# Sparse attention and a hardswish feed-forward block on one core: all engines' operations in another listed order

## The chip, the core and the metric

The kernel runs on one core of a Trainium2 chip. The metric is the time of one execution on the device, in microseconds (us); a lower time is better. The engines are named as the profile names them: PE (TensorE, matmuls), DVE (VectorE), ACT (ScalarE), POOL (GpSimd) and SP (SyncE), the last of which only starts transfers here. PEld is the weight load of PE.

## What is computed

Four batches of eight heads, 768 rows and 64 columns go through an attention over a local window and over one summary per block of 32 keys. Its result is the input of a feed-forward block with 512 inputs, 2048 hidden columns and a hardswish gate. Cut to what matters, the reference is:

```python
# q, k, v: (4, 8, 768, 64); w_in: (512, 2048); w_out: (2048, 512)
k_sum = k.reshape(B, H, 24, 32, D).max(axis=3)
v_sum = v.reshape(B, H, 24, 32, D).mean(axis=3)
scores_l = where(|i - j| < 16, q @ k.T / 8, -1e9)
scores_s = q @ k_sum.T / 8 + log(32)
a = softmax(concat([scores_l, scores_s]))
x = a @ concat([v, v_sum])                    # heads side by side: (3072, 512)
h = x @ w_in
out = (h * clip(h + 3, 0, 6) / 6) @ w_out     # (3072, 512), float32
```

## The kernel before, in words

The rows are worked off in eight tiles of 384 rows, s = 0 to 7: two halves of each batch. Each tile goes through attention (scores, exp, masking, values), is turned into x, and then through sixteen blocks of the first matrix (F) and three blocks of rows of the second (G).

**Nothing is scheduled by loops at run time.** The loops of the program only register operations under short keys such as `F5x2.0`, with the engine, the operation and the operations it depends on. The method `Plan.issue` then walks through the text `ORDER` and emits the operations one after the other. Every engine takes its instructions in that listed order, so `ORDER` alone decides what stands ahead of what in each engine's queue. A suffix `:A` or `:D` chooses ACT or DVE for a copy that either could do. Buffers are given out while the text is read: an operation that needs a new buffer gets the free one that was left longest ago.

```python
for n, token in enumerate(ORDER.split()):
    if token[0] in "~-_=":
        keep(...)                      # matmuls on a constant tile, result unused
        continue
    ...
    b.pool, b.slot = min(((p, s) for p in b.among for s in self.pools[p]), key=lambda x: since[id(x[1])])
    ...
```

The keys that matter below:

- `K0a`, `Q0g`, `V0c`, `Q0wu`: loads of batch 0, issued on POOL: keys (`K02` is twice the size of `K00` and `K01`), the queries of the second half row-wise (`Q00`, `Q01`), values by pair of heads, and the queries of the first half in wide rows. `I..` and `O..` are the two weight matrices, `K1..`, `Q1..`, `V1..` and so on the later batches.
- `c.N`: constants. `c.1` builds the identity matrix on POOL, `c.2` the window on POOL, `c.6` and `c.7` the ones beside the values, `c.8` to `c.11` clear the rows of the values that come from the block before.
- `kP`, `qG`: transposes of keys and queries on PE (lines 391, 420, 441) with their copies on ACT or DVE and the maximum over each block on DVE (line 402).
- `sBPH`: scores and exp (lines 489 and 495 for batch 0, 512 and 520 later) and the masking (lines 497, 521); the second digit is the pair of heads (batch 0) or a group of them, the third the half.
- `uN`: block sums of the values (lines 535 and 553) and their spreading; `hBPX`: copies of values of the block before.
- `v0P`: the values of tile 0 by pair of heads (line 581), scaling (598, 605), transposes (589) and the copy into x. `v4HG` is the second half of batch 0, and `vBHG` batch B: values (623), scaling, and for batch 1 transposes (636). From tile 4 on, x is made in another way: the scaled values are turned in blocks of 32 on DVE (`.3`, line 642, into y), and SP moves them by sixteen transfers (`.4` to `.7` of the group that stands second, line 648) into x. F of a tile waits for all sixteen.
- `FSxN.0` is one block of the first matrix, four matmuls of 384 columns (line 666), `.1` the relu on ACT (line 670), `.2` the gate on DVE (line 671). Three PSUM banks h serve F, so the fourth F waits for the gate of the first. For tile 0 the blocks 0 to 4 are split into four single matmuls.
- `GSTxA.0` to `.3` is one block of rows of the second matrix, four matmuls of 512 columns each (line 683), into one PSUM bank o; `.4` is the copy out and `.5` the store, issued on SP (lines 693, 694). The last block of all is split into halves of columns, and its end is copied half by ACT and half by DVE (lines 699 to 703).
- `~N`, `_N`, `-N`, `=N`: matmuls on the constant tile `idle` (line 782) that fill time on PE: N of 512, 64 or 128 columns, and for `=N` one of N times 64.

Of the kernel before, what the change touches and what calls it, by code (L numbers as in the profile page):

```python
# [37 lines left out]
F0x8.1 F0x8.2 F0x5.1 I0.0 F0x5.2 F0x11.0 F0x1.0 F0x11.1 F0x11.2 F0x1.1 F0x1.2 F0x1.3 F0x1.4 F0x1.5 v410.0 v410.1 F0x7.0 F0x7.1
F0x7.2 v410.2 F0x10.0 F0x10.1 I12.0 F0x13.0 F0x13.1 F0x15.0 F0x15.1 F0x13.2 F0x10.2 v411.3 v411.4:D v410.3 v410.4:A F0x15.2
F0x14.0 F0x14.1 F0x14.2 F0x9.0 F0x9.1 F0x9.2 F0x0.0 F0x0.1 F0x2.0 F0x2.1 K13.0 K10.0 c.12:A F0x0.2 K12.0 K11.0 w10.0 Q1w1.0  # L40
F1x14.0 F1x14.1 F1x14.2 F1x4.0 F1x4.1 F1x4.2 F1x2.0 F1x2.1 F1x2.2 w10.1:D F0x2.2 F0x2.3 F0x2.4 F0x12.0 F0x12.1 F0x12.2 F1x8.0
F1x8.1 F1x8.2 F1x1.0 F1x1.1 F1x1.2 F0x0.3 F0x0.4 F0x0.5 F0x2.5 F1x9.0 F1x9.1 F1x9.2 F1x5.0 F1x5.1 F1x5.2 F1x15.0 F1x15.1 w11.0
w11.2 F1x15.2 w11.3:D Q1w4.0 Q1w2.0 Q1w0.0 w10.2 w10.3:D q6.0 q6.1:A q7.0 q7.1:A F1x7.0 F1x7.1 w11.1:A F1x7.2 F1x12.0 F1x12.1
F1x12.2 O0.0 G02x0.0 Q1w5.0 Q1w3.0 q4.0 q4.1:A q5.0 q5.1:A F1x6.0 F1x6.1 F1x6.2 O1.0 G02x0.1 s100.0 s100.1 s100.3 F1x3.0 w12.0
F1x11.0 F1x11.1 w13.0 w13.2 F1x3.1 F1x11.2 w12.2 w12.1:D O2.0 G02x0.2 s101.0 s101.1 O3.0 F1x10.0 G02x0.3 G02x0.4:A w13.3:D
w13.1:A s101.3 F1x0.0 G00x0.0 G00x0.1 w12.3:D s100.2 s101.2 s100.4 V10.0 h100.0:D F1x10.1 h110.0:A F1x10.2 F1x3.2 s110.0 s110.1
s110.2 s101.4 s110.3 G00x0.2 G00x0.3 G00x0.4:A V12.0 u4.0 h130.0:D h120.0:A F1x0.1 u4.1:D u4.2:A u4.4:D u4.3:D u4.5:D G02x0.5
G01x0.0 G01x0.1 G01x0.2 s110.4 F1x0.2 h111.0:A v100.0 v100.1 v100.2 h121.0:A v101.0 v101.1 v101.2 G01x0.3 G01x0.4:A K20.0 K21.0
K22.0 K30.0 K23.0 w21.0 F1x13.0 F1x13.1 F1x13.2 v100.3 v100.4:A w20.0 w21.3 G12x0.0 w21.2:A v101.3 v101.4:A V22.0 H2.0 h101.0:A
w20.3 G12x0.1 G12x0.2 F2x2.0 F2x2.1 F2x11.0 F2x2.2 F2x11.1 F2x11.2 s111.0 w23.0 s111.3 F2x1.0 F2x1.1 F2x1.2 F2x3.0 F2x3.1 F2x3.2  # L50
F2x15.0 F2x15.1 F2x15.2 Q22.0 w23.3 G12x0.3 s111.1 G12x0.4:A F2x5.0 F2x5.1 h131.0:A F2x5.2 F2x6.0 G10x0.0 s111.2 w22.0 w22.3
s111.4 w23.4:A V20.0 H2.1:A K33.0 F2x13.0 F2x13.1 F2x13.2 G10x0.1 F2x6.1 F2x0.0 F2x0.1 F2x0.2 u5.0 u5.1:A u5.5:A F2x6.2 v110.0
v111.0 v111.1 v111.2 Q30.0 F2x4.0 F2x4.1 F2x4.2 Q21.0 Q23.0 Q20.0 w22.4:A F2x10.0 F2x10.1 F2x10.2 F2x12.0 F2x12.1 w20.1 F2x12.2
w22.2:A v110.1 w21.4:A Q33.0 Q32.0 G10x0.2 G01x0.5 G10x0.3 G10x0.4:A v110.2 F2x8.0 F2x8.1 w21.1 w20.2:A F2x9.0 w20.4:A F2x9.1
F2x9.2 u5.2:D F2x14.0 u5.4:D w23.2:A F2x8.2 v111.3 F2x14.1 v111.4:A G11x0.0 G11x0.1 u5.3:D w22.1 v110.3 v110.4:A F2x7.0 F2x7.1
G11x0.2 F3x14.0 F3x14.1 F2x14.2 F2x7.2 F3x14.2 s200.0 s200.1 w23.1 w21.5:A s200.3 G11x0.3 F3x9.0 F3x9.1 F3x9.2 F3x8.0 F3x8.1
F3x8.2 F3x13.0 Q31.0 K31.0 s200.4 s200.2 G11x0.4:A G11x0.5 G12x0.5 s210.0 s210.3 s210.4 s210.1 s210.2 F3x4.0 F3x12.0 G22x0.0
F3x13.1 F3x13.2 H3.0 v201.0 K32.0 V32.0 w20.5:D F3x4.1 F3x4.2 V30.0 G00x0.5 F3x12.1 v200.0 v200.1 F3x2.0 v201.1 v201.2 v201.3
G22x0.1 F3x0.0 F3x0.1 G22x0.2 G22x0.3 w23.5:A G22x0.4:A F3x12.2 v200.2 v200.3 v201.5 F3x1.0 F3x1.1 F3x1.2 s201.0 w31.0 G20x0.0
v201.4 F3x0.2 F3x2.1 s201.3 F3x2.2 F3x11.0 s201.1 G20x0.1 F3x5.0 F3x11.1 F3x3.0 F3x5.1 F3x11.2 w30.0 F3x5.2 v201.7 F3x15.0  # L60
G20x0.2 F3x15.1 F3x15.2 w30.3 F3x3.1 F3x3.2 w22.5:A w30.4:D s201.4 F3x6.0 F3x6.1 H3.1:A G20x0.3 G20x0.4:A F3x7.0 F3x10.0 G21x0.0
s211.0 F3x7.1 F3x10.1 s201.2 F3x7.2 s211.3 s211.1 F3x10.2 w32.0 F3x6.2 w32.3 s211.4 s211.2 w30.2:A G21x0.1 G21x0.2 G21x0.3
G21x0.4:A u6.0 u6.1:D u6.5:A u6.4:A u6.2:A w31.3 v211.0 v201.6 v210.0 v210.1 v210.2 w31.2:D v211.1 v210.3 v211.2 v211.3 G10x0.5
w31.4:D w33.0 G32x0.0 G32x0.1 G32x0.2 G32x0.3 G32x0.4:A F4x14.0 F4x14.1 F4x14.2 F4x4.0 F4x4.1 w32.2:A F4x4.2 F4x15.0 F4x15.1
F4x15.2 w31.1 G30x0.0 G30x0.1 F4x8.0 F4x8.1 F4x8.2 F4x2.0 F4x2.1 F4x2.2 F4x13.0 G30x0.2 F4x13.1 u6.3:A F4x13.2 w33.3 F4x7.0
F4x7.1 F4x7.2 G21x0.5 G20x0.5 v211.4 F4x6.0 F4x6.1 F4x6.2 v211.7 v211.6 v211.5 w30.1 F4x11.0 F4x11.1 F4x11.2 G30x0.3 G30x0.4:A
G30x0.5 F4x1.0 F4x1.1 w33.2:A F4x1.2 w32.4:D F4x5.0 F4x5.1 F4x5.2 G22x0.5 s300.0 s300.3 s300.1 F4x3.0 F4x12.0 F4x12.1 F4x9.0
F4x3.1 F4x9.1 w31.5:A w33.4:A w33.1 w32.1 F4x9.2 F4x12.2 w32.5:D s300.2 G31x0.0 G31x0.1 G31x0.2 s300.4 F4x3.2 s310.0 s310.3
s310.4 s310.1 s310.2 F4x0.0 F4x0.1 F4x0.2 F4x10.0 G31x0.3 w30.5:A F4x10.1 w33.5:D F4x10.2 v301.0 v301.1 v300.0 v301.2 v300.1
G31x0.4:A G31x0.5 v300.2 v300.3 v301.3 F5x14.0 F5x14.1 v301.5 v301.7 v301.6 v301.4 F5x2.0 G42x0.0 G42x0.1 F5x1.0 F5x1.1 F5x2.1  # L70
G42x0.2 F5x14.2 F5x1.2 F5x2.2 s301.0 s301.3 G42x0.3 G42x0.4:D s301.1 s301.2 F5x6.0 F5x6.1 F5x6.2 F5x4.0 F5x4.1 F5x4.2 F5x3.0
s311.0 s311.3 s311.4 F5x9.0 F5x9.1 F5x9.2 F5x3.1 F5x3.2 s311.1 s311.2 s301.4 G40x0.0 F5x13.0 F5x5.0 F5x5.1 F5x0.0 G40x0.1
F5x13.1 F5x13.2 F5x5.2 F5x0.1 F5x0.2 v310.0 v311.0 F5x10.0 v310.1 v310.2 F5x7.0 F5x7.1 F5x7.2 v311.1 F5x8.0 F5x8.1 F5x8.2
F5x10.1 F5x10.2 G40x0.2 F5x12.0 G40x0.3 G40x0.4:A G42x0.5 F5x15.0 F5x11.0 v310.3 v311.2 v311.3 v311.7 F5x11.1 G32x0.5 G41x0.0
G41x0.1 G41x0.2 F5x11.2 F5x15.1 F5x15.2 F6x14.0 F5x12.1 F5x12.2 F6x14.1 F6x14.2 F6x12.0 F6x12.1 F6x12.2 F6x9.0 F6x9.1 F6x9.2
G41x0.3 G41x0.4:A F6x10.0 F6x10.1 F6x7.0 F6x4.0 F6x4.1 F6x10.2 G52x0.0 F6x4.2 F6x7.1 F6x7.2 F6x8.0 F6x8.1 F6x1.0 F6x8.2 F6x1.1
F6x1.2 F6x0.0 F6x0.1 F6x0.2 G52x0.1 F6x3.0 F6x11.0 F6x11.1 G52x0.2 F6x3.1 F6x3.2 G52x0.3 G52x0.4:D F6x5.0 F6x5.1 F6x11.2 F6x2.0
F6x2.1 F6x5.2 F6x2.2 G51x0.0 F6x13.0 F6x13.1 F6x6.0 F6x15.0 G51x0.1 v311.6 F6x6.1 F6x6.2 F6x15.1 v311.5 v311.4 F7x5.0 F6x15.2
F6x13.2 F7x5.1 F7x5.2 F7x13.0 F7x9.0 F7x13.1 F7x13.2 F7x9.1 F7x9.2 G51x0.2 F7x12.0 F7x12.1 F7x12.2 F7x10.0 F7x10.1 F7x10.2
F7x1.0 G51x0.3 F7x1.1 F7x1.2 G51x0.4:A F7x3.0 G40x0.5 F7x6.0 F7x6.1 F7x6.2 G51x0.5 F7x8.0 F7x8.1 F7x8.2 G62x0.0 F7x4.0 F7x4.1  # L80
F7x4.2 F7x3.1 F7x3.2 F7x2.0 G62x0.1 F7x15.0 F7x2.1 F7x2.2 F7x15.1 F7x15.2 F7x0.0 G62x0.2 F7x0.1 G62x0.3 F7x7.0 F7x7.1 F7x0.2
# [732 lines left out]
```

## Time and profile before

| | before |
|---|---|
| time of three runs, us | 217.43, 216.99, 216.66; median 216.99 |
| span of the profiled execution, first to last instruction, us | 215.4 |
| PE busy, us | 207.6 (96%) |
| DVE busy, us | 162.1 (75%) |
| ACT busy, us | 136.0 (63%) |
| POOL busy, us | 49.7 (23%) |
| PE matmuls, instructions | 2521 recorded |
| mean granted clock of PE | 0.998 of full speed |

The profiled execution has no time of its own beside its span; the median lies 1.6 us above the span. Busy time of PE counts the matmuls on the constant tile too. All times in the views below are counted from the start of the span.

### The profile page before, as it was taken

To read this page: it belongs to the slowest core of one execution; us is meant where nothing else is said; L and a number is where in the kernel's file an instruction comes from. 1 tells how busy PE (TensorE), PEld (TensorE's weight loads), DVE (VectorE), ACT (ScalarE), POOL (GpSimd) and SP (SyncE) were. 2 spreads that over 40 slices of the span, in tenths; PEclk is the share of its full clock that TensorE was granted. 3 is DMA by queue.
4 is the path that set the end of the run, shared out by engine and by line. 5 is a ranking of instruction groups with operands and counts; after the bars stand their busy time and mean duration, and the time that the engine had idled before them with its cause. 6 is when DMAs were issued, how large, how long until landed. Compare 5 with 4: busy or idle time off the path is not lost.

```text
span 215.4 us, 6065 instructions
## 1 busy us (share of the span) xinstructions
PE 207.6 (96%) x2521; PEld 119.9 (56%) x2548; DVE 162.1 (75%) x318; ACT 136.0 (63%) x264; POOL 49.7 (23%) x66
## 2 busy tenths in 40 slices
PE   7999999999999999999999999999999999999993
...
DVE  6889889999899999898899889887865555640021
...
PEclk9999999999999999999999999999999999999999
...
DMA packets 91724, 22.68 MB, mean 105 GB/s; under 512 B 82224, under 2 KB 88752, under 8 KB 91696
## 3 DMA queue, kind: packets, MB, share of 16 engines
...
q1 hardware_dynamic: 29264, 7.80, 15.3%
...
## 4 chain that ended last, share of the span: by engine, by line
PE 82%; SPq 5%; DMA 4%; issue 2%; DVE 2%; POOL 2%; ACT 1%; ACTq 0%; POOLq 0%
PE h L666 36%; PE o L683 29%; PE h L683 5%; SPq L648 4%; DMA first<-in_q_dram 3%; PE S L623 3%; PE S L512 2%; DMA out_dram<-ot 1%; ACT vaug L241 1%; POOL first L305 1%; PE S L636 1%; PE S L666 1%; PE h L581 1%; PE S L489 1%; PE S L553 1%
## 5 line engine op out<-in xcount | busy, mean ns | idle before, releaser
L666 PE MATMUL h<-x,win 128*128 128x384 bf16 x500 | 91.1, 326 | 0.1
L670 ACT ACTIVATE r<-h 128x384 f32<-128x384 f32 x125 | 58.7, 492 | 38.8 <-PE h L666 36.8
L671 DVE SCALAR_TENSOR_TENSOR g<-r,h 128x384 bf16<-128x384 f32 x125 | 65.9, 546 | 22.6 <-ACT r L670 20.0
L683 PE MATMUL o<-wout,g 128*128 128x512 bf16 x309 | 78.0, 379 | 1.9 <-issue 0.8
L666 PEld LDWEIGHTS <-win 128*128 128x128 bf16 x512 | 48.7, 98 | 35.5
L683 PEld LDWEIGHTS <-g 128*128 128x128 bf16 x400 | 38.4, 98 | 37.6 <-issue 0.3
L520 ACT ACTIVATE at<-S 120x768 bf16<-120x768 f32 x24 | 18.6, 810 | 5.5 <-PE S L512 5.4
L241 ACT COPY ot<-o 128x512 f32<-128x512 f32 x17 | 10.0, 587 | 15.4 <-PE o L683 14.2
L521 DVE TENSOR_TENSOR at<-at,mask 96x768 bf16<-96x768 bf16 x24 | 12.6, 549 | 2.0 <-ACT at L520 1.6
L605 DVE TENSOR_TENSOR xn<-S,rc 128x768 bf16<-128x768 f32 x14 | 13.3, 950 | 0.3
L343 POOL DMA_DIRECT2D vaug<-in_v_dram x10 | 11.9, 1194 | 0.4 <-DMA first<-in_k_dram 0.2
L241 DVE COPY ot<-h 128x512 f32<-128x512 f32 x2 | 1.3, 686 | 13.7 <-PE h L683 13.7
L683 PE MATMUL h<-wout,g 128*128 128x256 bf16 (+1 forms) x64 | 11.4, 326 | 0.0
L467 DVE TENSOR_REDUCE red<-kaug 128x24 bf16<-128x768 bf16 x12 | 11.2, 943 | 0.1
L241 ACT COPY vaug<-vaug 32x640 bf16<-32x640 bf16 (+3 forms) x17 | 8.9, 574 | 0.6 <-DMA vaug<-in_v_dram 0.3
L241 ACT COPY vaug<-vs 24x1536 bf16<-24x1536 bf16 x6 | 8.8, 1468 | 0.6 <-DVE vs L241 0.5
L782 PE MATMUL o<-idle 128*128 128x64 bf16 (+2 forms) x70 | 7.5, 287 | 1.1 <-DVE idle L287 1.1
L455 DVE STREAM_TRANSPOSE kaug<-kraw 128x768 bf16<-128x768 bf16 x8 | 8.1, 1025 | 0.3 <-PE S L512 0.3
L623 PEld LDWEIGHTS <-at 120*64 120x64 bf16 x336 | 6.3, 111 | 3.0 <-issue 1.6
...
L642 DVE STREAM_TRANSPOSE y<-xn 128x768 bf16<-128x768 bf16 x8 | 7.6, 965 | 0.2
L512 PEld LDWEIGHTS <-kaug 32*128 32x128 bf16 x576 | 5.3, 92 | 4.4 <-issue 3.6
...
## 6 DMA issues: line engine op xcount, KB each, us to landing
...
vaug<-in_v_dram POOLq DMA_DIRECT2D x6, 384.0 KB, 12.9
...
win<-in_moe_w_in_dram POOLq DMA_DIRECT2D x3, 512.0 KB, 10.0
kraw<-in_k_dram POOLq DMA_DIRECT2D x8, 192.0 KB, 12.4
x<-y SPq DMA_DIRECT2D x64, 24.0 KB, 2.0
first<-in_k_dram POOLq DMA_DIRECT2D x6, 192.0 KB, 12.3
first<-in_q_dram POOLq DMA_DIRECT2D x6, 192.0 KB, 12.3
```

The lines of the kernel that those rows point to most:

```text
L241: {"ACT": nc.scalar.copy, "DVE": nc.vector.tensor_copy, "POOL": nc.gpsimd.tensor_copy}[eng](o, i)
L343: op("POOL", "dma128", lambda: nc.gpsimd.dma_start(out=o[BLK:WIN, a:z, 0:D], in_=rows[:, a:z]), w=[("v", b % 2, c) for c in range(lo, hi)] ...
L467: op("DVE", "max", lambda: nc.vector.tensor_reduce(red.slot[:], w[:, :, BLK:WIN].rearrange("p t (n c) -> p t n c", n=2), axis=AX.X, op=ALU ...
L512: nc.tensor.matmul(X[g // 2].slot[:, g % 2, i * QB:(i + 1) * QB], kaug[2 * u + m][rows, t], qT[rows, 2 * u + m, t * QB:(t + 1) * QB], star ...
L520: op("ACT", "exp", lambda a=a, e=e: nc.scalar.activation(a, X[e].slot[0:KEYS, :, 0:HALF], AF.Exp, scale=scl), r=[X[e]], w=[("at", p, half)])
L521: op("DVE", "masking", lambda m=m: nc.vector.tensor_tensor(m, m, mask[:, low(half):low(half) + HQ].unsqueeze(1).to_broadcast([WIN, 2, HQ, ...
L605: nc.vector.tensor_tensor(o, src[..., 0:D], r.unsqueeze(len(r.shape)).to_broadcast(list(o.shape)), op=ALU.mult)
L623: nc.tensor.matmul(X.slot[64 * c:64 * c + 64, i, m:m + D + 1], a[:, t * QB:(t + 1) * QB], vaug[b % 2][0:KEYS, h, t, 0:D + 1], start=True, ...
L666: nc.tensor.matmul(bank(h)[:, 0:HALF], w_in_sb[:, kt, cols], xt[s].slot[:, kt], start=(kt == 0), stop=(kt == NP - 1))
L670: op("ACT", "relu", lambda: nc.scalar.activation(r.slot[:], bank(h)[:, 0:HALF], AF.Relu, bias=0.5, scale=1.0 / 6.0), r=[h], w=[r])
L671: op("DVE", "gate", lambda: nc.vector.scalar_tensor_tensor(gt[s].slot[:, ft], r.slot[:], 1.0, bank(h)[:, 0:HALF], op0=ALU.min, op1=ALU.mul ...
L683: nc.tensor.matmul(o.slot[:, a:z], gt[s].slot[:, ft, ts * 128:(ts + 1) * 128], w_out_sb[:, ft, a:z], start=(ft == 0), stop=(ft == NFT - 1))
```

## The change

The program's functions are the same. `ORDER` is replaced by another text with the same 960 operations, each once, and 13 filling tokens in both, of other sizes. What differs:

- the loads of batch 0 come in the order K01, Q00, K02, K00, V01, V00, Q0w2, Q0w0, Q0w1, Q01, V02, V03, in place of K00, K01, K02, Q00, Q01, V00 to V03, Q0w0 to Q0w2; the identity is built after the window and not before it;
- all constants, copies and steps of tile 0 are interleaved in another way; every F of tile 0 now stands behind all of x of that tile;
- the two value steps of batch 0's second half, `v411.0` and `v410.0`, stand next to each other on PE; before, four F stood between them;
- fewer matmuls on the constant tile: 9 of 512 columns in place of 19, 13 of 128 in place of 15, and 40 of 64 in both;
- 53 copies, spreads and clears change sides between ACT and DVE;
- the sequence of F and G in all tiles, and where the stores and the moves of x stand on SP, are different.

The text has one line more, so that line numbers of the changed kernel are one higher. The diff, cut to the places named here and in the prediction:

```diff
-c.0 K00.0 c.7 c.17 c.6 c.8:A K01.0 c.10:D c.5 c.1 _40 -15 k0.0 k0.2:A c.18 ~1 =2 k1.0 K02.0 ~12 =3 k2.0 k3.0 c.15:D c.2 c.3
-s000.0 k0.3:A c.13:D c.4 c.11:A k1.1 Q00.0 q0.0 k1.4 k0.1 c.20 k1.2:A Q01.0 ~2 =5 q1.0 k0.4 k1.3:D c.9:A c.14:A c.19 k2.3:A
...
-s021.1 s011.1 s021.2 v03.4 v03.5:D s011.2 v02.5:A s031.0 s031.1 s001.0 s031.2 I2.0 F0x3.0 F0x3.1 F0x3.2 F0x3.3 F0x3.4 F0x3.5
-I4.0 F0x6.0 F0x6.1 F0x6.2 F0x4.0 F0x4.1 F0x4.2 F0x4.3 v411.0 v411.1 F0x5.0 F0x4.4 F0x4.5 v411.2 s001.1 I8.0 u0.2:A s001.2 F0x8.0
...
+c.0 c.18 K01.0 Q00.0 K02.0 c.2 c.4 c.1 _40 -13 k1.0 k1.2:A c.3 K00.0 c.6 V01.0 ~1 =6 q0.0 c.19 c.10:A c.11:A k1.3:A c.20 q0.2:A
+k1.1 c.17 q0.1:D V00.0 ~5 =4 k2.0 k3.0 s010.0 k2.2:A c.9:A k2.1 k1.4 c.5 k0.0 s010.1 k0.1 k0.4 s010.2 k3.2:A k2.3:A k0.3:A
+k0.2:D c.16 c.8:D s030.0 k3.1 Q0w2.0 Q0w0.0 Q0w1.0 ~1 =5 s000.0 Q01.0 V02.0 V03.0 I4.0 I8.0 I12.0 k3.3:A h000.0:D =7 s000.1
+u0.0 u0.3:A h010.0:D u0.1:A u0.4:D s000.2 ~1 =7 q3.0 v01.0 k2.4 v01.1 q3.1:D q2.0 I2.0 s021.0 k3.4 v01.2 q2.1:D v01.3 q1.0
+q1.2:D v00.0 v00.1 v01.4 s030.1 h001.0:A s021.1 h011.0:A s020.0 q1.1:D v00.2 s020.1 s030.2 s020.2 v01.5:D v00.3 I0.0 Q1w4.0
+K11.0 K10.0 Q1w2.0 Q1w5.0 h020.0:D c.7 u1.0 u1.1:A u1.3:A v00.4 v02.0 v02.1 s001.0 s031.0 h021.0:A h030.0:D s031.1 u1.4:D v03.0
+v03.1 v02.2 v02.3 u0.2:D v02.4 s011.0 v03.2 v03.3 s001.1 v02.5:A v00.5:D v03.4 v03.5:D ~1 =4 F0x7.0 F0x6.0 F0x5.0 u1.2:D s021.2
+s011.1 h031.0:A s031.2 s001.2 K12.0 K13.0 Q1w3.0 F0x7.1 s011.2 F0x6.1 F0x7.2 F0x6.2 F0x5.1 v411.0 v410.0 v411.1 F0x5.2 v411.2
...
+G31x0.4:A s310.3 s310.4 s310.2 F4x7.0 F4x15.0 G42x0.0 F4x7.1 F4x8.1 v211.4 v300.0 v301.0 F4x7.2 F4x8.2 v301.1 F4x15.1 G42x0.1
+F4x14.0 F5x0.0 F5x0.1 w30.5:A v300.1 v301.2 F4x14.1 w33.5:A v300.2 w31.5:A F4x15.2 F5x0.2 F4x14.2 v300.3 G42x0.2 F5x2.0 F5x14.0
+F5x2.1 s311.0 s311.1 F5x14.1 F5x9.0 G32x0.5 G20x0.5 F5x2.2 v301.3 F5x14.2 F5x9.1 F5x9.2 G42x0.3 F5x15.0 G42x0.4:A F5x11.0
+F5x8.0 G30x0.5 F5x15.1 G40x0.0 F5x11.1 s311.3 s301.0 F5x8.1 F5x15.2 F5x8.2 F5x4.0 s301.3 F5x4.1 F5x4.2 G40x0.1 F5x11.2 s301.1
+s311.2 G40x0.2 v301.7 v301.4 G31x0.5 F5x13.0 G40x0.3 F5x13.1 s301.4 s311.4 s301.2 F5x12.0 F5x12.1 v311.0 F5x13.2 G40x0.4:A
+G42x0.5 v311.1 v311.2 v310.0 F5x5.0 F5x5.1 F5x5.2 F5x12.2 F5x3.0 F5x3.1 F5x3.2 G41x0.0 F5x1.0 F5x6.0 F5x6.1 F5x6.2 F5x1.1
+F5x1.2 v310.1 v311.3 G41x0.1 v301.6 v301.5 F6x12.0 F6x6.0 F6x12.1 F6x6.1 F6x6.2 F6x12.2 v310.2 v310.3 G41x0.2 G41x0.3 G41x0.4:A
...
```

More of the change, by code (lines that the diff above doesn't have):

```diff
@@ L38 @@
[L38 to L81, printed above, removed]
@@ new lines @@
+v03.1 v02.2 v02.3 u0.2:D v02.4 s011.0 v03.2 v03.3 s001.1 v02.5:A v00.5:D v03.4 v03.5:D ~1 =4 F0x7.0 F0x6.0 u1.2:D s021.2 F0x5.0
+s011.1 h031.0:A s031.2 s001.2 K12.0 K13.0 Q1w3.0 F0x7.1 s011.2 F0x6.1 F0x7.2 F0x6.2 F0x5.1 v411.0 v410.0 v411.1 F0x5.2 v411.2
+F0x11.0 Q1w0.0 F0x11.1 F0x11.2 F0x9.0 F0x9.1 F0x9.2 F0x8.0 v410.1 v411.3 F0x15.0 F0x13.0 v411.4:A F0x2.0 F0x2.1 F0x2.2 v410.2
+v410.3 F0x2.3 F0x15.1 Q1w1.0 F0x15.2 F0x13.1 F0x8.1 F0x13.2 F0x8.2 F0x14.0 F0x3.0 F0x3.1 F0x2.4 F0x2.5 F0x14.1 F0x14.2 F0x3.2
@@ new lines @@
+F0x10.0 F0x1.0 v410.4:A F0x3.3 F0x10.1 F0x3.4 F0x1.1 F1x11.0 c.14:A F0x4.0 F0x4.1 O0.0 F0x4.2 F0x1.2 F1x11.1 F0x3.5 F0x10.2
+F1x11.2 F0x1.3 F0x4.3 F0x4.4 F1x13.0 F0x4.5 F1x13.1 F1x13.2 F1x3.0 F1x14.0 O1.0 F0x1.4 F0x1.5 F1x3.1 F1x14.1 F1x14.2 F1x3.2
+F0x0.0 F1x9.0 F0x0.1 F1x9.1 F0x0.2 F0x0.3 O2.0 O3.0 F1x1.0 F1x9.2 F0x0.4 F1x1.1 F0x0.5 F1x1.2 F1x10.0 F0x12.0 F0x12.1 F1x10.1
+q6.0 q7.0 w11.0 F0x12.2 w10.0 F1x10.2 V12.0 F1x7.0 F1x8.0 G02x0.0 F1x5.0 q6.1:A F1x7.1 F1x8.1 F1x8.2 c.15:A w11.1:A F1x0.0
```

44 lines of the change are left out of this document (36 added, 8 removed).

## The prediction

> **What bounds the kernel now.** I read the page first: busy times, the slices, the granted clock.
>
> ```profile
> span 215.4 us, 6065 instructions
> PE 207.6 (96%) x2521; PEld 119.9 (56%) x2548; DVE 162.1 (75%) x318; ACT 136.0 (63%) x264; POOL 49.7 (23%) x66
> PE   7999999999999999999999999999999999999993
> DVE  6889889999899999898899889887865555640021
> PEclk9999999999999999999999999999999999999999
> ```
>
> PE is full in all slices but the first and the last, at full clock; DVE is nearly full for the first 28 slices (150 us). So I asked when PE gets to its main work and whether it waits afterwards: the timeline of PE around the first F, and what PE waited for from 24.3 us to the end; the last two rows, from the chain of waits, give the step from one matmul to the next in a full stream.
>
> ```profile
> 1.13 3.92 PE L782 MATMUL o<-idle 128*128 128x64 bf16 x55 [1.13 <-DVE idle L287]
> 21.32 0.26 PE L581 MATMUL h<-vaug,at 96*64 96x65 bf16 x5 [0.31 <-issue]
> 24.39 2.12 PE L666 MATMUL h<-x,win 128*128 128x384 bf16 x12
> 26.45 0.47 PE L623 MATMUL S<-vaug,at 120*64 120x65 bf16 x18
> PE o L683 <- issue: 0.8, 5, 0.2
> PE S L623 <- issue: 0.3, 1, 0.3
> 119.78 1.73 PE o L683 x8
> 121.51 1.95 PE h L666 x12
> ```
>
> The first F starts at 24.39. After it PE never waits for another engine or a transfer: only 1.1 us of "issue" are left. One F (four matmuls of 1.95/12 = 0.1625) takes 0.65, one part of G (four of 1.73/8 = 0.216) 0.86. I compared the two listed orders at that point: ahead of the first F stand the same operations of PE (all key and query transposes of batch 0, its eight scores, two sums, all four values of tile 0), and behind it the same 282, without filling in either. The result is therefore the shift of the first F, plus new waits behind it, minus switches saved. Before has nearly nothing to lose there, so a gain must come from the start, and each clash the new order has is a loss.
>
> **The start.** Each transfer's issue (timeline of POOL, or the chain of waits) and its time to landing:
>
> ```profile
> 1.36 1.42 POOL L305 DMA_DIRECT2D first<-in_k_dram  x2 [0.84 <-POOLq L798]
> first<-in_k_dram POOLq DMA_DIRECT2D x1, 192.0 KB, 3.4
> 3.32 0.73 POOL L305 DMA_DIRECT2D first<-in_k_dram  x1
> first<-in_k_dram POOLq DMA_DIRECT2D x1, 384.0 KB, 5.4
> 4.76 1.34 POOL L312 DMA_DIRECT2D first<-in_q_dram  x2
> first<-in_q_dram POOLq DMA_DIRECT2D x1, 192.0 KB, 5.7
> 5.43 7.02 DMA first<-in_q_dram
> 8.90 1.03 POOL L343 DMA_DIRECT2D vaug<-in_v_dram  x1
> vaug<-in_v_dram POOLq DMA_DIRECT2D x1, 192.0 KB, 8.3
> 12.73 0.88 POOL L325 DMA_DIRECT2D qwide<-in_q_dram  x1 [0.58 <-DMA first<-in_q_dram]
> qwide<-in_q_dram POOLq DMA_DIRECT2D x1, 128.0 KB, 7.0
> ```
>
> Landings of before (issue plus time to landing) are K00 4.8, K02 8.7, Q00 10.5, Q01 12.4, V03 17.2, last of Q0w 19.7: one stream, so its steps can be put in another order. Between K00 and K02 lie K01 and K02, three shares of 192 KB in 3.9: K01 1.3, K02 2.6. Q00 costs 1.7 to 1.8, Q01 2.0, a V 1.2, all of Q0w 2.5. In the new order: K01 4.8, Q00 6.5, K02 9.2, K00 10.4, V01 11.6, V00 12.8, Q0w 15.3, Q01 17.3, V02 18.5, V03 19.7. The last values come 2.5 us later, the wide queries 4.4 us earlier.
>
> From there I walked the new order forward by hand, with these durations beside the matmul rows (the groups of instructions; the copies have PE to ACT or DVE handoffs of some 0.05):
>
> ```profile
> L402 DVE TENSOR_REDUCE red<-h 128x24 bf16<-128x768 bf16 x3 | 2.8, 949 | 0.4 <-PE h L391 0.4
> L495 ACT ACTIVATE at<-S 120x768 bf16<-120x768 f32 x8 | 6.3, 810 | 1.2 <-PE S L489 1.1
> L282 DVE MEMSET vaug<- 32x768 f32 x3 | 2.1, 698 | 0.4 <-issue 0.2
> L241 ACT COPY vaug<-vaug 32x640 bf16<-32x640 bf16 x6 | 4.3, 717 | 0.0
> L605 DVE TENSOR_TENSOR xn<-h,rc 128x384 bf16<-128x384 f32 x4 | 2.1, 555 | 0.1
> 17.67 0.85 PE L535 MATMUL o<-vaug,ind 96*32 96x128 bf16 x24
> ```
>
> Keys 2 and 3 are transposed from 9.3 to 10.2. DVE then has their and key 0's maxima, the block indicators, a copy of key 0 and the clear `c.8` (0.95+0.95+0.7 and 1.6 of copies), to 14.1, and `u0` needs that clear: 14.2 to 15.0 on PE. Q3, the values of pair 1, Q2, a score, then Q1 (landing 17.3) to 18.0, the values of pair 0 to 18.6, three scores to 19.75. V03 has landed at 19.7: `u1` to 20.6. Behind it stand five short steps and two scores, to 22.1; the values of pair 3 to 22.7; ACT comes to the last exps and copies (eight of 0.7 to 0.8 since 15.6) at 24.0, DVE scales (0.56) to 23.5; the last transpose ends at 23.85 and its copy at 24.2. The first F would start at 24.3. One "issue" gap like the 0.31 at 21.32 fits into such a stretch, so I take 24.6: **+0.2**. Its bounds are 23.7 (V03 at 19.7 plus 4.0 of steps that can't overlap) and 25.8 (each of some twenty handoffs 0.06 slower than taken).
>
> **Switches.** Twelve matmuls of F from 24.39 at 0.1625 each end at 26.34, and the values start at 26.45: 0.11 for going to the other layout, the same for going back. `v411` and `v410` side by side save one pair: **−0.2**.
>
> **The moves of x.** Here the new order is tight. These rows are of tile 6: value steps, turns on DVE, sixteen moves on SP, first F; then three gates in a row, a store between moves, and the moves' landing.
>
> ```profile
> 136.24 0.95 PE L623 MATMUL S<-vaug,at 120*64 120x65 bf16 x48
> 139.52 1.84 DVE L642 STREAM_TRANSPOSE y<-xn 128x768 bf16<-128x768 bf16 x2
> 141.42 11.13 SPq L648 DMA_DIRECT2D x<-y  x16
> 159.19 2.11 PE L666 MATMUL h<-x,win 128*128 128x384 bf16 x12
> 157.34 1.48 DVE L671 SCALAR_TENSOR_TENSOR g<-r,h 128x384 bf16<-128x384 f32 x3
> 160.54 0.61 SPq L694 DMA_DIRECT2D out_dram<-ot  x1
> L648 SPq DMA_DIRECT2D x<-y x16: 591/618/1194, 141.4 to 151.9; - x16
> DMA to landing us min/median/max: 2.0/2.0/3.2
> ```
>
> Before: values end at 137.19, y is ready at 141.4, the last move starts at 151.9 and lands at 153.9, F starts 5.3 later. After: between the values of tile 6 and its first F stand 15 F, 9 parts of G and the same rest, in place of 16 and 11; at 0.65 and 0.86 that is 22.0 − 2.4 = 19.6 us until PE is there. DVE has four gates (two more if `F4x7` and `F4x8` are late) among the scalings and turns: 4.2 + 4×0.465 = 6.1, or 7.0. SP has two stores (`G31`, `G42`) between the moves: 10.5 + 1.2, and 2.0 to land. Sum 19.8 to 20.7, against 19.6: F waits 0.2 to 1.1, I take **+0.5**. The bounds are 0 (SP's moves at 0.66 as in other tiles and handoffs hidden) and 1.6 (a store's bytes ahead of a move, 3.2 in place of 2.0). By the same count tile 5 has 1 to 2 us to spare, tiles 4 and 7 two. [...]
>
> **Elsewhere.** I counted the DVE work listed ahead of each thing that PE needs from the first F on against PE's own work ahead of it: DVE never falls behind in either order, so single clashes remain. At `v100`, 5.0 us of PE work stand behind `u4`, and 4.2 us of DVE work plus handoffs. I take **+0.2** for all of these, from 0 to 1.5. At the end, DVE now copies its half first:
>
> ```profile
> 212.22 0.27 ACT L699 COPY ot<-h 128x128 f32<-128x128 f32 x1 [5.90 <-PE h L683]
> 212.52 0.29 DVE L702 COPY ot<-h 128x128 f32<-128x128 f32 x1 [0.90 <-ACT ot L699]
> ```
>
> DVE waited for ACT; after, ACT waits for DVE: 0.27 and 0.29 change places, 0. Ten fewer idle matmuls of 512 columns bring nothing by themselves: they stood where PE waited.
>
> Sum: 0.2 − 0.2 + 0.5 + 0.2 = +0.7 on the span, 215.4 to 216.1. The runs' median lies 1.6 above the span: 216.99 + 0.7 = 217.7.
>
> **Rivals.**
> 1. The moves come in time and nothing clashes: +0.2 − 0.2 = 0, 217.0. For it: tile 6 misses by less than the error of my handoffs. Against it: it needs every one of the tight places to hold.
> 2. Faster: PE work alone sets the start. The matmuls listed behind key 0's transpose are some 10 us, so from 10.4 PE could be done by 21, and only V03's tail holds it to 23.7: −0.7. With the switches −0.2, and without the 0.3 of "issue" in `v411`, 215.8. It decides if ACT and DVE run a us ahead of my walk; against it stands ACT, which has no pause from 15 to 24.
> 3. Slower in the start: the DVE queue from 9.9 to 14.1 is a single chain of maxima and copies, and `u0`, the exps and all later slots of S hang on it. At the bound of 25.8, +1.4, with tile 6's wait 218.9.
> 4. Slower by the clock: 10 fewer 512-column fillings leave PE idle between 8 and 9.3 and in four shorter places; if the clock were halved there for as long as the first fillings last (3.92 at 1.13), 2.0 us of work comes later, 219.0. Against it: before shows full clock from its first slices, with 1.1 idle at the start. [...]
>
> That the order does not change is no rival: hardly an instruction of PE keeps its neighbours.
>
> **Numbers.** A change below 0.3% (0.65 us) can't be told from none here. Forecast 0.42 (its own range 217.2 to 219.0; 0.32 of it above 217.64, 0.10 within), rival 1 0.25, rival 2 0.17, rival 3 0.13, rival 4 0.03. Slower 0.32+0.13+0.03 = 0.48, same 0.35, faster 0.17. The range from 216.1 to 219.3 leaves out most of rival 2 and the upper ends of 3, under 0.2.
>
> **What would show it.** First F at 24.6 in PE's timeline (23.7 for rival 2, 25.8 for 3); `v411` and `v410` as one piece of 48; in PE's waits a wait of the first F of tile 6 for the x moves, with SP's last move after PE's last G; no "half clock" in the first slices. A wait of over 1 us anywhere else, or a first F outside 23.7 to 25.8, proves the sum wrong.

## The result, and the profile after

The changed kernel takes 228.07 us (median of four runs, 226.92 to 228.44), the kernel before 216.82 beside it (215.99 to 217.43): a ratio of 1.050, interval 1.046 to 1.054. Forecast were 217.7 and a range of 216.1 to 219.3: slower, as forecast, but by sixteen times the 0.7 us of the sum. The profiled execution took 228.44 with a span of 226.7. The page first:

```profile
span 226.7 us, 6029 instructions
PE 213.5 (94%) x2509; PEld 123.5 (54%) x2536; DVE 158.4 (70%) x308; ACT 135.2 (60%) x274; POOL 49.3 (22%) x66
PE   7578999999999999999999999999989999999994
DVE  2356668789899999999889799785867454334100
PEclk9955558999999999999999999999999999999999
```

In the line of the granted clock stands what no step of the sum had: fives and an eight from the third slice to the seventh. Twelve recorded matmuls fewer than before, and PE is busy 5.9 us longer. The view by windows of time, cut where the clock changes (its column PEclk comes third from the right), gives the stretch:

```profile
8.82:12.23 3.41, 1.59 (x50) 1.21 (x50) 1.49 (x4) 1.06 (x3) 2.70 (x4) 1.00 1.96 166
12.30:36.10 23.80, 21.19 (x307) 13.99 (x302) 16.54 (x43) 14.54 (x33) 15.33 (x20) 0.50 1.79 183
36.20:220.00 183.80, 180.51 (x2046) 101.38 (x2072) 138.00 (x251) 114.31 (x230) 23.63 (x27) 1.00 0.72 87
```

From 12.2 to 36.1 us the clock is at half. In that time PE was busy for 21.19 of 23.80 us, so it had work most of the time and worked at half its speed. Just ahead of the fall it had been busy for 1.59 of 3.41 us. By the trace's clock record the half clock lasted seven times 3.413 us and the full clock ahead of it twice that; a stretch of 3.413 us is called a window below. The timeline of PE gives the milestones of the forecast:

```profile
10.64 0.87 PE L392 MATMUL h<-ident,first 96*64 96x96 bf16 x32 [2.63 <-DMA first<-in_k_dram]
...
18.13 0.82 PE L536 MATMUL o<-vaug,ind 96*32 96x128 bf16 x12 [0.52 <-DVE vaug L283]
...
33.73 3.29 PE L667 MATMUL h<-x,win 128*128 128x384 bf16 x12
36.96 0.95 PE L624 MATMUL S<-vaug,at 120*64 120x65 bf16 x48
...
127.31 0.81 PE L667 MATMUL h<-x,win 128*128 128x384 bf16 x4 [0.31 <-DMA x<-y]
168.24 1.46 PE L667 MATMUL h<-x,win 128*128 128x384 bf16 x8 [0.55 <-DMA x<-y]
```

Keys 2 and 3 come at 10.64 (walk: 9.3), `u0` at 18.13 (walk: 14.2), the first F at 33.73 (forecast: 24.6, bounds 23.7 to 25.8). So 9.3 of the 11.3 us by which the span grew lie ahead of the first F. The waits of PE (in all, times, longest) point at two of the causes:

```profile
PE h L392 <- DMA first<-in_k_dram: 2.8, 2, 2.6
PE S L490 <- DVE kaug L242: 1.1, 1, 1.1
PE h L667 <- DMA x<-y: 0.9, 2, 0.6
```

The first is the landing of `K02`. The second is behind `u0`'s lateness; the timeline of DVE and ACT shows what DVE itself waited for (in square brackets, idle time and releaser):

```profile
11.88 0.96 DVE L403 TENSOR_REDUCE red<-h 128x24 bf16<-128x768 bf16 x1 [1.93 <-ACT kaug L242]
...
14.29 1.97 ACT L242 COPY kaug<-h 128x576 bf16<-128x576 bf16 x7
...
16.30 0.76 DVE L242 COPY kaug<-h 128x576 bf16<-128x576 bf16 x1 [1.54 <-ACT kaug L242]
...
17.38 0.70 DVE L283 MEMSET vaug<- 32x768 f32 x1 [0.19 <-issue]
```

DVE stood idle twice until ACT had copied. `k2.1` and `k2.2:A` read the same tile of PSUM, and so do `k0.2:D` and `k0.3:A`; the list has ACT's reader first in both pairs, and DVE's begins 0.03 to 0.04 after ACT's ended. `k0.2:D` could have begun at 14.75, right behind `k0.4`; it began at 16.30, and `s000.1`, the clear `c.8` (17.38) and `u0` moved with it. The walk let both engines read at once. The two copies at the end show the same thing, which the prediction had seen there and only there:

```profile
223.44 0.29 DVE L703 COPY ot<-h 128x128 f32<-128x128 f32 x1 [12.61 <-PE h L684]
223.76 0.27 ACT L700 COPY ot<-h 128x128 f32<-128x128 f32 x1 [1.06 <-DVE ot L703]
```

In each of these pairs the second reader began 0.03 to 0.04 us after the first had ended; whether the two could read at once, no run here shows.

So there are three suspects, the landing, the readers' order and the clock, and the first two can feed the third: a late chain leaves holes in PE.

### The profile page after: what moved, and what is told of

It is laid out like the page before. It is cut to its first block, busy times and chain, and to the rows that moved or that the text cites. A ratio compares the mean times of both kernels' runs of the same rounds, so it can differ in the third digit from the quotient of the medians.

```text
span 226.7 us, 6029 instructions
## 1 busy us (share of the span) xinstructions
PE 213.5 (94%) x2509; PEld 123.5 (54%) x2536; DVE 158.4 (70%) x308; ACT 135.2 (60%) x274; POOL 49.3 (22%) x66
## 4 chain that ended last, share of the span: by engine, by line
PE 83%; SPq 5%; DMA 4%; issue 2%; DVE 2%; ACT 2%; POOL 1%; DVEq 0%; POOLq 0%
PE h L667 34%; PE o L684 29%; PE h L684 5%; SPq L649 4%; DMA first<-in_k_dram 3%; PE S L624 2%; PE S L513 2%; PE h L582 2%; PE S L490 1%; PE S L667 1%; ACT kaug L242 1%; PE S L554 1%; PE S L637 1%; DMA x<-y 1%; DVE red L403 1%
## 5 line engine op out<-in xcount | busy, mean ns | idle before, releaser
L667 PE MATMUL h<-x,win 128*128 128x384 bf16 x496 | 92.5, 329 | 0.9 <-DMA x<-y 0.9
L672 DVE SCALAR_TENSOR_TENSOR g<-r,h 128x384 bf16<-128x384 f32 x124 | 64.4, 544 | 30.8 <-ACT r L671 29.4
L667 PEld LDWEIGHTS <-win 128*128 128x128 bf16 x512 | 49.3, 99 | 38.8 <-issue 3.0
L521 ACT ACTIVATE at<-S 120x768 bf16<-120x768 f32 x24 | 18.8, 810 | 3.6 <-PE S L513 3.4
L242 ACT COPY ot<-o 128x512 f32<-128x512 f32 x18 | 10.5, 586 | 12.3 <-PE o L684 12.2
L684 PE MATMUL h<-wout,g 128*128 128x512 bf16 (+1 forms) x64 | 10.9, 326 | 0.0
L242 ACT COPY vaug<-vaug 32x640 bf16<-32x640 bf16 (+3 forms) x20 | 9.9, 547 | 0.3 <-DVE red L468 0.2
L242 ACT COPY kaug<-h 128x480 bf16<-128x480 bf16 (+3 forms) x15 | 4.7, 400 | 8.7 <-PE h L392 6.0
L496 ACT ACTIVATE at<-S 120x768 bf16<-120x768 f32 x8 | 6.4, 810 | 4.2 <-PE S L490 4.2
## 6 DMA issues: line engine op xcount, KB each, us to landing
win<-in_moe_w_in_dram POOLq DMA_DIRECT2D x3, 512.0 KB, 10.1
```

Source lines behind the costliest of these rows:

```text
L242: {"ACT": nc.scalar.copy, "DVE": nc.vector.tensor_copy, "POOL": nc.gpsimd.tensor_copy}[eng](o, i)
L521: op("ACT", "exp", lambda a=a, e=e: nc.scalar.activation(a, X[e].slot[0:KEYS, :, 0:HALF], AF.Exp, scale=scl), r=[X[e]], w=[("at", p, half)])
L667: nc.tensor.matmul(bank(h)[:, 0:HALF], w_in_sb[:, kt, cols], xt[s].slot[:, kt], start=(kt == 0), stop=(kt == NP - 1))
L672: op("DVE", "gate", lambda: nc.vector.scalar_tensor_tensor(gt[s].slot[:, ft], r.slot[:], 1.0, bank(h)[:, 0:HALF], op0=ALU.min, op1=ALU.mul ...
L684: nc.tensor.matmul(o.slot[:, a:z], gt[s].slot[:, ft, ts * 128:(ts + 1) * 128], w_out_sb[:, ft, a:z], start=(ft == 0), stop=(ft == NFT - 1))
```

## The experiments

All are edits of the listed order. `~N` is N fillings of 512 columns. First F, `u0` and clock are from each run's profiled execution. Ratios are to the kernel before on the same chip, where its median was 217.3 to 217.8.

**One hole filled** (`fill_one`), in the changed kernel:

```
- ... V00.0 ~5 =4 k2.0 k3.0 ...
+ ... V00.0 ~17 =4 k2.0 k3.0 ...
```

> The changed kernel with twelve more 512-column matmuls on the constant tile ahead of the transposes of keys 2 and 3 (~17 in place of ~5), which fill the 2.6 us in which PE waited for K02. Theory 1 (the clock: that hole lets the granted clock fall to half from 12.2 to 36.1 us, and the half clock is the loss): mean clock back to 0.99, first F at 25 to 27 us in place of 33.7, 218 to 220 us. Theory 2 (late loads and the queue of DVE set the start, the clock is a companion): first F still at 30 us or later, 224 to 228 us.

Measured: 227.99 us, ratio 1.048 (1.043 to 1.052). The hole of 2.63 is gone, but the clock fell later, at 17.71, and was back at 34.78; first F 33.77. `s000.1` and `u0` came at 16.92 and 17.94. From the transposes of keys 2 and 3 to `u0` it took 7.33 us, nearly all of it at full clock, and 7.49 in the change, most of it at half: `u0` doesn't hang on the clock. The holes ahead of `s000.1` and `u0` (1.99 and 0.67 us) left PE little to do just ahead of the fall:

```profile
14.30:17.71 3.41, 0.98 (x15) 0.47 (x15) 1.74 (x5) 1.77 (x7) 3.30 (x6) 1.00 2.14 167
```

The single hole is not the cause by itself.

**The same hole in the kernel before** (`before_hole`):

```
- ... K02.0 ~12 =3 k2.0 ...
+ ... K02.0 ~1 =3 k2.0 ...
```

> The kernel before with ~1 in place of ~12 in front of the transposes of keys 2 and 3: a hole of some 2.4 us on PE from 7.1 to 9.6, everything else as before. Theory 1: the clock falls to half at the end of that window and stays there until F runs; first F at 29 to 34 us, 223 to 228 us. Theory 2: nothing but the idle matmuls is missing, 217 us within 0.5.

Measured: 219.28 us over six runs. Five of them lie between 217.88 and 220.57, ratio 1.007 (1.003 to 1.011); the sixth took 224.17, with a mean granted clock of 0.959. In the profiled one (220.57) the hole was 3.25 us long, as `K02` landed only at 10.0, and the first F came at 27.66 in place of 24.39. By windows:

```profile
4.60:7.90 3.30, 2.05 (x41) 1.12 (x38) 2.75 (x8) 2.26 (x6) 3.30 (x5) 1.00 1.03 144
8.00:18.20 10.20, 8.19 (x111) 4.52 (x111) 6.30 (x18) 6.15 (x13) 8.01 (x11) 0.50 2.10 156
```

Here too the clock falls, at the end of a stretch in which PE was busy 2.05 of 3.30 us; but in this order it comes back by itself at 18.2, ahead of the first F, so the missing fillings cost 0.7% in five runs of six, and some 3% in the sixth, less than the 5% of the change. Neither theory had that: the fall is there, but it doesn't last to F.

**The landing of K02** (`eye_as_before`: the identity is made ahead of `K02`'s issue; `k02_first`: `K02` issued ahead of `Q00`):

```
- ... K01.0 Q00.0 K02.0 c.2 c.4 c.1 _40 ...
+ ... K01.0 Q00.0 c.1 K02.0 c.2 c.4 _40 ...
```

> The changed kernel with the identity built on POOL ahead of the issue of K02 and not behind the window, as the kernel before has it. If POOL's constants behind the issue are what made K02 land at 10.6 in place of the 9.2 that I had worked out, K02 lands at 9.3 to 9.8, the hole on PE shrinks to about 1.5 us; theory 1 then says that the clock holds or not by where the window's edge lies: 218 to 219 us with the clock held, 226 or more without. Theory 2: 1 us less than the changed kernel, 226 to 227 us.

```
- c.0 c.18 K01.0 Q00.0 K02.0 ... ~1 =6 q0.0 ... k1.3:A c.20 q0.2:A ... q0.1:D V00.0 ...
-   k2.0 k3.0 s010.0 k2.2:A c.9:A ...
+ c.0 c.18 K01.0 K02.0 Q00.0 ... ~1 =6 ... k1.3:A c.20 ... V00.0 ...
+   k2.0 k3.0 q0.0 s010.0 q0.2:A k2.2:A c.9:A q0.1:D ...
```

> The changed kernel with K02 issued ahead of Q00, and the transpose of Q00 behind those of keys 2 and 3 on PE. K02 lands at 8.7 to 9.2 and Q00 at 10.5. Theory 1: the hole on PE is under 1 us, the clock holds, 217.5 to 219.5 us. Theory 2: the start is 1.5 us earlier, 226 us.

The transfers of a short stretch of time list the issue to landing; first the changed kernel (issue at 2.84), then `fill_one` (also at 2.84), then `k02_first` (issue at 2.12):

```profile
first<-in_k_dram POOLq DMA_DIRECT2D x1, 384.0 KB, 7.8
```

```profile
first<-in_k_dram POOLq DMA_DIRECT2D x1, 384.0 KB, 6.8
```

```profile
first<-in_k_dram POOLq DMA_DIRECT2D x1, 384.0 KB, 6.1
```

`K02` landed at 10.6, 9.73 (`eye_as_before`) and 8.2 us. The times were 227.05 and 227.3, ratios 1.044 (1.041 to 1.047) and 1.043 (1.037 to 1.049); first F 32.94 and 32.88; `u0` 17.31 and 17.26. Both are near what theory 2 had. In `eye_as_before` `u0` and the first F came 0.8 us earlier than in the change, with a landing 0.9 us earlier.

That the identity's place made the difference is not shown. Five other runs keep POOL's list of the change, and in their profiles `K02` landed at 9.6 (`fill_one`), 9.7 (`readers`), 9.9 (`fill_all`), 10.1 (`readers_fill`) and 10.5 (`lift`): the landing of one and the same list differs by 1 us from execution to execution, and `eye_as_before` lies inside that spread. With POOL's list of the kernel before it was 8.7 there, 9.0 in `pair_alone` and 10.0 in `before_hole`.

The landing at 8.2 in `k02_first` moved `u0` by only 0.05 more, but its edit also put the copies of `q0` ahead of key 2's maximum on DVE, and there DVE waited for ACT:

```profile
10.40 0.56 DVE L242 COPY qT<-o 128x384 bf16<-128x384 bf16 x1 [1.20 <-ACT qT L242]
```

It came to key 2 at 10.94, as it had at 11.01 in `eye_as_before`. So this run does not show what the earlier landing alone is worth.

**The readers' order** (`readers`), only the places of DVE's readers:

```
- ... k1.0 k1.2:A ... q0.2:A k1.1 c.17 ... k2.2:A c.9:A k2.1 ... k2.3:A k0.3:A k0.2:D ...
+ ... k1.0 k1.1 k1.2:A ... q0.2:A c.17 ... k2.1 k2.2:A c.9:A ... k2.3:A k0.2:D k0.3:A ...
```

> The changed kernel with three moves in the list and nothing else: the maxima of keys 1 and 2 (k1.1, k2.1, on VectorE) stand ahead of the ScalarE copies that read the same PSUM tile, and k0.2:D ahead of k0.3:A. Theory A (two engines that read one PSUM tile are held in the listed order, and this keeps s000.1 and u0 back): s000.1 at 14.8 to 15.6 us instead of 17.1, u0 at 15.7 to 16.5 instead of 18.1, first F 1.6 to 2.4 us earlier, at 31.3 to 32.1; the clock still falls to half at about 12 us, since nothing fills PE's holes, and stays there to the first F; 225.5 to 226.5 us. Rival B (u0 is late because matmuls at half clock are slow): u0 and first F as in the changed kernel, 33.7, and 228 us.

The timeline of `readers`, and below it that of `eye_as_before`, whose keys 2 and 3 were transposed at the same time:

```profile
9.78 0.87 PE L390 MATMUL h<-ident,first 96*64 96x96 bf16 x32 [1.34 <-DMA first<-in_k_dram]
11.42 0.64 ACT L240 COPY kaug<-h 128x576 bf16<-128x576 bf16 x1 [1.49 <-DVE red L401]
15.04 0.51 PE L534 MATMUL o<-vaug,ind 96*32 96x128 bf16 x12 [0.55 <-DVE vaug L281]
30.16 3.99 PE L665 MATMUL h<-x,win 128*128 128x384 bf16 x12
```

```profile
9.77 0.87 PE L392 MATMUL h<-ident,first 96*64 96x96 bf16 x32 [1.88 <-DMA first<-in_k_dram]
...
17.31 0.82 PE L536 MATMUL o<-vaug,ind 96*32 96x128 bf16 x12 [0.52 <-DVE vaug L283]
```

Now ACT waits for DVE, and from the same 9.8 us `u0` follows 2.27 us earlier. Theory A holds, and B falls. The first F came at 30.16, earlier than I had expected: the clock fell only at 16.9. The hole ahead of key 2 was 1.34 us here, as `K02` had landed at 9.7. The four runs fall into two pairs: 225.40 and 225.75 with a mean granted clock of 0.962, and 219.95 and 221.61 with 0.992 and 0.984 (the ratio of 1.014, 1.005 to 1.023, is of the second pair alone). One and the same order thus comes out some 5 us apart, and the time goes with the mean clock. The profiled run is one of the first pair, and its windows hold the most surprising row of the study, the second:

```profile
6.70:16.80 10.10, 6.67 (x128) 4.03 (x129) 7.06 (x21) 7.73 (x21) 9.59 (x13) 1.00 1.98 158
17.00:30.10 13.10, 13.08 (x238) 9.71 (x237) 9.54 (x25) 9.36 (x19) 5.81 (x8) 0.50 1.49 196
30.20:33.90 3.70, 3.70 (x13) 1.62 (x11) 3.15 (x7) 1.64 (x4) 2.85 (x4) 0.50 2.09 169
```

From 17.0 to 30.1, up to the first F, PE was busy for 13.08 of 13.10 us, and the clock stayed at half. Idleness isn't what keeps it there. From 30.16 on PE ran F, and the clock was back at 34.0.

**All holes filled** (`fill_all`), the order of the real work as in the change, and **both** (`readers_fill`):

```
- ... ~5 =4 k2.0 ... ~1 =5 s000.0 ... =7 s000.1 u0.0 ... ~1 =7 q3.0 ...
+ ... ~17 =4 k2.0 ... ~4 =5 s000.0 ... ~6 =7 s000.1 ~3 u0.0 ... ~2 =7 q3.0 ...
```

> The changed kernel with fillings in each hole of PE between 8 and 20 us (17 wide ones ahead of k2, 3 more ahead of s000.0, 6 ahead of s000.1, 3 ahead of u0, one more ahead of q3), the order of all real work as in the changed kernel. Theory (the clock falls where PE has holes or little work in a window, and most of the loss is the half clock): the clock stays full through the whole start; s000.1 and u0 stay at 17 and 18 us, since they hang on VectorE and ScalarE; first F 28 to 29.5 us instead of 33.7, 221 to 223 us. Rival (the loss is the order of the readers and landings, the clock a consequence): first F at 33 again, 227 us or more. If the clock still falls in a window in which the narrow matmuls leave no hole, it is their shape and not idleness that lets it fall.

`readers_fill` has the three moves of `readers`, and 2 fillings each ahead of `s000.1` and `u0` in place of 6 and 3.

> Both: the three moves of the readers and fillings in the holes (17 wide ones ahead of k2, 3 more ahead of s000.0, 2 ahead of s000.1, 2 ahead of u0, one more ahead of q3). If the two causes make up the loss between them: clock full, u0 at 15.7 to 16.5, first F at 25.5 to 27, 218.3 to 220 us, that is within 1.2% of the kernel before. If the clock falls all the same, first F at 31 and 225 us.

`fill_all`, by windows:

```profile
6.50:29.80 23.30, 20.56 (x391) 12.81 (x391) 15.23 (x40) 16.09 (x38) 15.27 (x20) 1.00 1.68 178
```

The clock stays full. `u0` comes at 18.27, no earlier than in the change, the first F at 29.85 in place of 33.73; 223.16 us, ratio 1.025 (1.021 to 1.030), both just above what I had expected. The 17 fillings were too many by about 1 us: `K02` had landed at 9.9, and PE came to keys 2 and 3 at 10.92, straight from a filling. From there to `u0` it took 7.35 us (7.49 in the change). `readers_fill`, timeline of PE:

```profile
15.98 0.51 PE L533 MATMUL o<-vaug,ind 96*32 96x128 bf16 x12
...
27.48 2.11 PE L664 MATMUL h<-x,win 128*128 128x384 bf16 x12
```

Full clock too, first F 27.48; 220.99 us, ratio 1.017 (1.010 to 1.023). That is a little above both upper bounds I had set (27 and 220), but one cure on top of the other brings the first F 3.9 us forward by the clock and 2.4 by the readers. Of these 2.4, 0.5 is the earlier start of keys 2 and 3 (10.45 against 10.92), the rest the step from there to `u0` (5.53 against 7.35). From the first F to PE's end it takes 187.6 us, as in before (187.75): behind the first F, with full clock and no wait for `x`, the new order loses nothing.

**Lifting the clock afterwards** (`lift`): the change with only the later fillings of `fill_all`, so that the clock falls as it did.

```
- ... =7 s000.1 u0.0 ... ~1 =7 q3.0 ...
+ ... ~6 =7 s000.1 ~3 u0.0 ... ~2 =7 q3.0 ...
```

> The changed kernel with its fall of the clock left alone (no filling more ahead of k2 or s000.0) and wide fillings only behind it: 6 ahead of s000.1, 3 ahead of u0, one more ahead of q3, some 10 us of slots at half clock of 0.45 each, so 4 to 5 us of work that adds nothing. Theory (a window full of wide matmuls lifts the clock again, a window full of narrow ones doesn't): the clock falls at about 12 us and rises at the end of the first window full of fillings, at 19 to 20 us; u0 comes at 18.5 to 20, later than in the changed kernel, and the first F all the same earlier, at 30.5 to 32.5 instead of 33.7; 224 to 226.5 us. Rival (only the first F's own work lifts it, or a fall lasts a fixed time): the clock stays half to the first F, which comes at 34.5 to 35.5, and the time is 229 us or more.

Windows, then the timeline of PE:

```profile
12.20:18.90 6.70, 6.15 (x46) 2.57 (x41) 4.64 (x12) 3.04 (x10) 6.02 (x8) 0.50 2.22 164
19.00:29.90 10.90, 10.22 (x267) 7.43 (x267) 8.53 (x26) 9.47 (x21) 4.56 (x7) 1.00 1.39 201
```

```profile
15.37 3.14 PE L782 MATMUL o<-idle 128*128 128x512 bf16 x7
...
19.64 0.85 PE L535 MATMUL o<-vaug,ind 96*32 96x128 bf16 x24
...
29.90 2.11 PE L666 MATMUL h<-x,win 128*128 128x384 bf16 x12
```

The clock rose at 18.95, behind the first stretch full of wide fillings, and stayed up through the same narrow matmuls that leave it down in the change. `u0` is 1.5 us later than in the change, the first F 3.8 us earlier: 223.35 us, ratio 1.028 (1.026 to 1.030), better than I had expected. Matmuls that compute nothing made the kernel 2% faster than the change. The rival (only F lifts it, or a fall has a fixed length) falls.

**A version with everything** (`best_try`): `readers_fill` with `K02` and `q0` placed as in `k02_first`, fillings to match (11 ahead of `k2`, 1 ahead of `u0`), and `c.8` and `c.16` in DVE's idle time ahead of key 2.

```
- c.0 c.18 K01.0 Q00.0 K02.0 ... k1.3:A c.20 ... k2.3:A k0.2:D k0.3:A c.16 c.8:D s030.0 ...
+ c.0 c.18 K01.0 K02.0 Q00.0 ... k1.3:A c.20 c.17 c.8:D c.16 ... k2.3:A k0.2:D k0.3:A s030.0 ...
```

> Both causes taken away and the landing too: K02 issued ahead of Q00 (q0 transposed behind k3), the maxima of keys 1 and 2 and k0.2:D ahead of ScalarE's copies, the clear c.8 and c.16 in VectorE's idle time ahead of key 2, fillings in the holes (11 wide ones ahead of k2, 4 ahead of s000.0, 2 ahead of s000.1, 1 ahead of u0). The chain then starts with K02 at 8.2 us instead of 10.1: s000.1 at 13.3 to 14, u0 at 14 to 14.5, which is where my hand walk had it, and the first F by the 11.5 us that lie between u0 and F in the run with both cures: 25.3 to 26.3 us; 217.7 to 219 us, from even with the kernel before to 0.7% above it. If the hand walk behind u0 was right too (10.1 us), the first F comes at 24.3 and the time is 217. If V03's landing at 19.7 us is the bound by now, the first F doesn't come before 26.5.

Measured: 219.55 us (218.59 to 220.66), ratio 1.011 (1.008 to 1.014): the best of the new order, and still slower than before. The expectation was too low again by 0.5 to 1 us, and the first reason is the fillings themselves. `K02` was issued at 2.14 and had landed at 7.2, but PE worked off fillings until 9.13, where the expectation had keys 2 and 3 at 8.2:

```profile
first<-in_k_dram POOLq DMA_DIRECT2D x1, 384.0 KB, 5.1
```

```profile
5.78 3.42 PE L780 MATMUL o<-idle 128*128 128x512 bf16 x14
9.13 0.87 PE L389 MATMUL h<-ident,first 96*64 96x96 bf16 x32
```

Behind them came DVE's chain:

```profile
9.70 0.96 DVE L400 TENSOR_REDUCE red<-h 128x24 bf16<-128x768 bf16 x1 [0.59 <-PE h L389]
10.89 0.56 DVE L239 COPY qT<-o 128x384 bf16<-128x384 bf16 x1 [0.23 <-ACT qT L239]
...
13.83 0.75 DVE L239 COPY kaug<-h 128x576 bf16<-128x576 bf16 x1
```

It runs from 9.70 to 14.58 without `c.8`, 4.9 us where the walk had 4.2 with it, one more pair of readers in it (`q0.2:A`, `q0.1:D`). `u0` starts at 15.46, straight behind a filling, the first F at 26.76. `V03` landed at 18.58 and isn't the bound. What this order would reach with fewer fillings ahead of keys 2 and 3 was not run.

**The adjacency alone** (`pair_alone`), in the kernel before:

```
- v411.0 v411.1 F0x5.0 F0x4.4 F0x4.5 v411.2 s001.1 I8.0 u0.2:A s001.2 F0x8.0 F0x8.1 F0x8.2 ... F0x1.5 v410.0 v410.1
+ F0x5.0 F0x4.4 F0x4.5 s001.1 I8.0 u0.2:A s001.2 F0x8.0 v411.0 v410.0 v411.1 F0x8.1 v411.2 F0x8.2 ... F0x1.5 v410.1
```

> The kernel before with one part of the change alone, the adjacency: v411.0 (with its scaling and transposes) is moved behind u0.2 and s001.2, and v410.0 next to it, as one piece of 48 matmuls. By my term of the switches 0.2 us less than the kernel before, 216.6 to 217.2 us, ratio 0.998 to 1.0; nothing moves in the start. Rival: the scalings of both heads come on VectorE together and some F waits for them, 0.2 to 0.5 us more.

Measured: 217.09 us, ratio 0.999 (0.997 to 1.001), no difference that its twelve runs show. The timeline of PE:

```profile
27.54 0.57 PE L622 MATMUL S<-vaug,at 120*64 120x65 bf16 x24
28.42 0.57 PE L622 MATMUL S<-vaug,at 120*64 120x65 bf16 x24 [0.30 <-DVE rc L597]
```

The two heads stand side by side, and the second waits 0.30 for DVE. The 0.2 us of the switch are neither shown nor excluded.

## Why the prediction was wrong

The bound was named rightly: the result is the shift of the first F for the most part. The first F was forecast 0.2 us late and came 9.3 us late. By profiled executions the way back goes 33.73 (the change), 29.85 (clock held), 27.48 (readers' order too), 26.76 (landing and clear too, with the fillings in its way), 24.6 (forecast).

- **Rival 4, the clock, was the largest cause (3.9 us ahead of the first F), with 0.03 as its chance and 2.0 us as its price.** The step that failed was "for as long as the first fillings last (3.92 at 1.13)": the fall lasted 23.9 us. Against it I had held that before shows full clock from its first slices; but before has fillings in just those holes, and `before_hole` shows that its clock falls without them. The first slice was misread as well: the trace's clock record of before begins only at 6.47 us, and the same 16 transposes take 0.85 at 4.98, as they do at half clock in `before_hole` (10.65), and 0.54 at 6.41:

```profile
4.98 0.85 PE L391 MATMUL h<-ident,first 96*64 96x96 bf16 x16
6.41 0.54 PE L391 MATMUL h<-ident,first 96*64 96x96 bf16 x16
```

By the clock record of the change, full and half stretches last 2, 7 and 56 times 3.413 us (5.41 to 12.23, 12.23 to 36.13, 36.13 to 227.27, just behind the last instruction). A window with PE busy for 1.59 of 3.41 us stood ahead of the fall, and in `readers` 13.08 of 13.10 us of work didn't restore the clock. The length of the longest hole didn't give that of the fall: 2.63 and 23.9 us in the change, 3.25 and 10.2 us in `before_hole`.

- **The walk of the start: `u0` at 14.2 was the step that failed next (1.8 to 2.3 us, from `readers_fill` against `fill_all` and `readers` against `eye_as_before`, both counted from keys 2 and 3).** It let ACT and DVE read one PSUM tile at the same time. Rival 3 had the right chain (DVE from 9.9 to 14.1) with a price of at most 1.4, since it put 0.06 on each handoff, and not ACT's copies of 0.6 to 2.0 us ahead of two of them.
- **The landing of `K02`**, worked out at 9.2, was 10.6 (0.8 us of the first F). From `Q00`'s landing it took 4.45 us in place of 2.7. In the five runs with the same list on POOL it took 3.4 to 4.5, and the 3.9 us from `K00` to `K02` in before, out of which the sum took its shares, were 4.1 in `pair_alone` and 5.2 in `before_hole`, with the same list: the shares had been read from one execution, and a short one. What lengthens it in one execution and not in another stays open. What stands behind it in the stream was late by as much, up to the wide queries; `Q01`, `V02` and `V03` (20.2, walk: 19.7) were within 0.5 us.
- **The rest, 2.2 us in `best_try`:** the chain on DVE 0.7 us longer than the walk, and `u0` 0.9 behind its end, with `s000.1` and fillings in between; `u0` in two halves because its second waits for a copy, and 10.0 us in place of 9.3 from `u0`'s end to the first F. The chain began at 9.7, with `K02` landed at 7.2, so the fillings also used up what the earlier landing had gained. These are from one trace and not taken apart further.
- **Moves of x: +0.5 at tile 6, measured 0.55**, with two stores between the moves, as worked out. Tile 4, which was to have two us to spare, waited too, 0.31. In the experiments this wait was 1.11 (`fill_all`, tile 4), 0.68 (`best_try`) and none (`readers_fill`), with one and the same order behind the start: so this term does not hang on the list alone. The 3.2 us behind its upper bound was not a store's: from 141.4 to 152 the trace of before has, beside the moves, only one transfer of instructions.
- **Switches −0.2:** the piece of 48 is there (36.96); its worth isn't shown. **Tail 0:** right. **Behind the first F** the change loses 1.9 us: 1.2 of half clock until 36.13 (2.4 us at half speed), 0.86 of waits for `x` and 0.3 for DVE, less some 0.5 of gains (among them the switch and an "issue" gap of 0.32 that before has in its values).
